# The start of a fused dynamic convolution and FFN: other load order, one read of w_in, other queues for the first rows, bands in pairs

## The chip, the cores and the metric

The kernel runs on one core of one Trainium2 chip. The metric is the device time of one execution in microseconds; several runs are taken and the median is quoted. A profile is one such execution; its span is some 1.9 us shorter than the run's time.

## The reference, cut to what matters

```python
# 8 x 4096 tokens of 192 channels; 8 heads of 24 channels; a 7-tap filter for each token and head
w = softmax(weight_gen, axis=-1)                    # (8, 4096, 8, 7)
x_unf = x_pad[:, idx, :].reshape(B, S, K, H, group)  # the token and the 6 before it
y = einsum('bshk,bskhg->bshg', w, x_unf).reshape(32768, 192)
h = maximum(y @ w_in, 0)                            # w_in 192 x 2048
out = (h * h) @ w_out                               # w_out 2048 x 192, float32 result
```

## The kernel before

The tokens are cut into 64 blocks of 512. For each block: DVE spreads the softmax weights over a band (`bd = wr * mask`), TensorE multiplies x with that band ("conv", PSUM `yp`), ACT copies it out as `y`, TensorE does FFN-in (`h`), ACT takes the relu (`t`), DVE squares it (`g`), and TensorE does FFN-out (`o`) half a block behind. Weights and the first two x blocks come as float32 and are cast on chip; later x blocks are cast by the DMA that POOL issues. Softmax rows are made by ACT and DVE, stored to DRAM (`vd`) and read back shifted (`wr`). Only the first rows go straight from SBUF to SBUF (`wr<-v_first`), as here:

```python
parts[0].load(nc.sync)                 # first softmax rows
x_load_f32(0)
parts[1].load(nc.sync)
load_w_in(0); load_w_in(1)             # each half of the partitions reads all of it: 2 x 384 KB a quarter
s0.exp(0, s0.rh); s1.exp(0, s1.rh)
s0.recip(0, s0.rh); s0.scale(0, s0.rh, nc.vector)
wr_load_sbuf(0, s0)                    # five copies, issued by SyncE
x_cast(0, act); x_load_f32(1)
cast_w_in(0, act); cast_w_in(1, act); load_w_in(2)
s1.recip(0, s1.rh); s1.scale(0, s1.rh, nc.vector)
wr_load_sbuf(1, s0)
load_w_in(3)
for q in range(WO):                    # WO = 4
    load_w_out(q)
    if q == 0:
        s0.store(nc.sync); s1.store(nc.sync)
        wr_load(2)
        for i in (2, 3): cast_w_in(i, pool)
    cast_w_out(q, pool)
parts[2].load(nc.sync)                 # third softmax rows
st_bands(0, BANDS); st_conv(0); st_y_evac(0)
x_cast(1, act); st_bands(1, BANDS)
x_load(2)                              # POOL, behind all the casts above
# ... then the loop over the 64 blocks
```

Each engine takes its own instructions in this order; semaphores order them across engines.

The softmax here doesn't subtract the row's maximum and nothing guards it: scores larger than these inputs give would overflow.

## Time and profile before

| what | value | from |
|---|---|---|
| time, median | 805.39 us (804.39 to 806.07, 4 runs) | runs |
| span of the profiled run, clock granted | 804.9 us, 0.984 | profile |
| TensorE busy from 104 to 780 us | 676 of 676 us | stretches |
| first FFN matmul | 21.02 us | time line |
| block 1's FFN starts | 47.18 us | time line |
| conv of block 3 starts | 59.40 us | time line |
| conv of block 4 ends | 76.46 us | chain |

The prediction shows the lines. The time line gives start, duration, engine, source line, operation and, in brackets, how long the engine was idle and who released it. The idle time that matters is TensorE's, and all of it lies in the first 80 us. The last three rows of the table are marks along the way to the steady part.

### The profile page before, as it was taken

To read this page: it belongs to the slowest core of one execution; us is meant where nothing else is said; L and a number is where in the kernel's file an instruction comes from. 1 tells how busy PE (TensorE), PEld (TensorE's weight loads), DVE (VectorE), ACT (ScalarE), POOL (GpSimd) and SP (SyncE) were. 2 spreads that over 40 slices of the span, in tenths; PEclk is the share of its full clock that TensorE was granted. 3 is DMA by queue.
4 is the path that set the end of the run, shared out by engine and by line. 5 is a ranking of instruction groups with operands and counts; after the bars stand their busy time and mean duration, and the time that the engine had idled before them with its cause. 6 is when DMAs were issued, how large, how long until landed. Compare 5 with 4: busy or idle time off the path is not lost.

```text
span 804.9 us, 32787 instructions
## 1 busy us (share of the span) xinstructions
PE 779.5 (97%) x14900; PEld 682.0 (85%) x14900; DVE 592.9 (74%) x1159; ACT 609.8 (76%) x757; POOL 70.3 (9%) x84
## 2 busy tenths in 40 slices
PE   7678999999999999999999999999999999999998
PEld 3466888888888888888888888888888888888887
DVE  5666878877777777887687777778778777666754
ACT  3556877787787787778778778777877877877785
POOL 3311000010000100001000100000000010000000
PEclk9779999999999999999999999999999999999999
DMA  8773253335343363333634354333533333433111
GB/s 203 192 141 55 62 130 66 70 63 142 62 75 51 63 154 51 68 68 65 140 62 74 52 142 74 51 65 72 142 63 63 70 55 88 74 50 63 49 41 41
DMA packets 125066, 66.70 MB, mean 83 GB/s; under 512 B 84609, under 2 KB 121088, under 8 KB 124160
## 3 DMA queue, kind: packets, MB, share of 16 engines
q1 hardware_dynamic: 83872, 49.18, 22.0%
q0 software_dynamic: 40784, 15.24, 18.0%
q8 instruction: 116, 1.90, 1.0%
q10 hardware_dynamic: 272, 0.20, 0.1%
q14 instruction: 22, 0.18, 0.1%
HBM read 50.31 MB, written 29.36 MB: 99 GB/s over the span
## 4 chain that ended last, share of the span: by engine, by line
PE 92%; DMA 4%; DVE 1%; SPq 1%; issue 1%; POOL 0%; ACT 0%; DVEq 0%; POOLq 0%
PE o L358 43%; PE h L339 43%; PE yp L315 7%; DMA w_st<-in_moe_w_in_dram 1%; DMA xt<-in_x_dram 1%; DMA vd<-v_first 1%; DMA wr<-v_first 1%; DVE bd L274 1%; DMA wo_st<-in_moe_w_out_dram 0%; POOL w_o L130 0%; SPq L114 0%; DVE g L375 0%; DVE v_big L188 0%; ACT ex L167 0%; DVE ssum L175 0%
## 5 line engine op out<-in xcount | busy, mean ns | idle before, releaser
L369 ACT ACTIVATE t<-h 128x1024 f16<-128x1024 f32 x512 | 483.1, 1029 | 10.8 <-PE h L339 10.2
L375 DVE TENSOR_TENSOR g<-t 128x1024 f16<-128x1024 f16 x512 | 346.9, 693 | 172.2 <-ACT t L369 171.9
L339 PE MATMUL h<-y,w_i 64*128 64x256 f16 x6144 | 365.2, 272 | 2.9 <-POOL w_i L118 1.5
L358 PE MATMUL o<-w_o,g 128*128 128x192 f16 x4096 | 360.8, 247 | 2.4 <-POOL w_o L130 2.4
L358 PEld LDWEIGHTS <-g 128*128 128x128 f16 x4096 | 331.9, 98 | 29.4 <-DVE g L375 17.3
L339 PEld LDWEIGHTS <-w_i 64*128 64x128 f16 x6144 | 294.1, 95 | 54.3 <-issue 12.4
L274 DVE TENSOR_TENSOR bd<-wr,mask 128x768 f16<-128x768 f16 (+2 forms) x320 | 170.0, 583 | 12.5 <-DMA wr<-vd 7.6
L328 ACT CAST y<-yp 128x768 f16<-128x768 f32 x64 | 51.1, 798 | 122.8 <-PE yp L315 122.8
L234 POOL DMA_DIRECT2D xt<-in_x_dram x55 | 47.5, 864 | 554.0 <-PE yp L315 519.4
L380 ACT COPY o_sb<-o 128x384 f32<-128x384 f32 x127 | 63.0, 496 | 38.4 <-PE o L358 38.4
L315 PE MATMUL yp<-bd,xt 128*32 128x96 f16 (+17 forms) x4608 | 61.7, 203 | 15.1 <-DMA xt<-in_x_dram 8.7
L315 PEld LDWEIGHTS <-xt 128*32 128x32 f16 (+3 forms) x4608 | 50.6, 91 | 26.6 <-issue 17.3
L175 DVE TENSOR_REDUCE ssum<-ex 128x64 f32<-128x448 f32 (+6 forms) x49 | 26.0, 530 | 16.6 <-ACT ex L167 16.2
L167 ACT ACTIVATE ex<-wg 128x448 f32<-128x448 f32 (+6 forms) x49 | 26.5, 540 | 14.8 <-DMA wg<-in_weight_gen_dram 14.8
L188 DVE TENSOR_TENSOR v_big<-ex,rcp 128x112 f16<-128x112 f32 (+3 forms) x192 | 32.8, 235 | 1.6
L180 DVE RECIPROCAL rcp<-ssum 128x64 f32<-128x64 f32 (+6 forms) x49 | 23.3, 476 | 1.7
L414 PE MATMUL wp<-warm 128*128 128x512 f16 x52 | 13.2, 422 | 1.3 <-DVE warm L408 1.3
L414 PEld LDWEIGHTS <-warm 128*128 128x128 f16 x52 | 5.5, 107 | 8.6 <-issue 2.5
L226 POOL DMA_DIRECT2D xt<-in_x_dram x7 | 3.9, 559 | 80.9 <-PE yp L315 80.9
L188 DVE TENSOR_TENSOR v_first<-ex,rcp 128x112 f16<-128x112 f32 (+2 forms) x32 | 5.5, 247 | 0.2
L232 POOL DMA_DIRECT2D xt<-in_x_dram x7 | 5.2, 748 | 0.0
L118 ACT CAST w_i<-w_st 128x1536 f16<-128x1536 f32 x2 | 2.9, 1472 | 2.9 <-DMA w_st<-in_moe_w_in_dram 2.9
(16 smaller groups left out, 19.7 us busy)
## 6 DMA issues: line engine op xcount, KB each, us to landing
out_dram<-o_sb SPq DMA_DIRECT2D x63, 384.0 KB, 2.7
xt<-in_x_dram POOLq DMA_DIRECT2D x55, 240.0 KB, 4.3
wg<-in_weight_gen_dram SPq DMA_DIRECT2D x6, 1064.0 KB, 6.4
wr<-vd SPq DMA_DIRECT2D x55, 80.0 KB, 2.9
vd<-v_big SPq DMA_DIRECT2D x7, 512.0 KB, 2.9
w_st<-in_moe_w_in_dram SPq DMA_DIRECT2D x8, 384.0 KB, 8.2
wo_st<-in_moe_w_out_dram SPq DMA_DIRECT2D x4, 384.0 KB, 4.2
xt<-in_x_dram POOLq DMA_DIRECT2D x7, 192.0 KB, 3.8
```

The lines of the kernel that those rows point to most:

```text
L167: nc.scalar.activation(out=self.ex[:, lo:hi].rearrange("p r g k e -> p (r g) k e"), in_=self.wg[:, lo:hi].rearrange("p r (g e) k -> p (r g ...
L175: nc.vector.tensor_reduce(out=ssum.rearrange("p r g e -> p (r g) e"), in_=self.ex[:, lo:hi].rearrange("p r g k e -> p (r g) e k"), axis=Ax ...
L188: eng.tensor_tensor(out=bass.AP(tensor=v.tensor, offset=v.offset + lo * H * SL + lo % SL * 2 + g * SL * 2, ap=[list(v.ap[0]), [H * SL + 2, ...
L234: eng.dma_start(out=dst, in_=rows(src, t0 + BASE, width))
L274: nc.vector.tensor_tensor(out=bd_t[j][:, H * lo : H * hi].rearrange("p (g m c) -> p g m c", g=HP, c=2 * SL), in0=wr_t[j][:, i].unsqueeze(2 ...
L315: nc.tensor.matmul(out=yp_t[j][p0 : p0 + m, col + a : col + b], lhsT=x_t[j][:, i, 32 * q : 32 * q + m], rhs=bd[:, h // 2, h % 2, a - lo : ...
L328: nc.scalar.copy(out=y, in_=yp_t[j][:, 0 : NK * TH].rearrange("p (k c) -> p k c", k=NK))
L339: nc.tensor.matmul(out=h[:, half, jj, :], lhsT=w_i[r0 : r0 + RT, k, fc * P : (fc + 1) * P], rhs=y_t[j][r0 : r0 + RT, k, :], start=(jj == 0 ...
L358: nc.tensor.matmul(out=o[half][:, cc * Dm : (cc + 1) * Dm], lhsT=g_t[(j, fp)][:, half, jj, cc * P : (cc + 1) * P], rhs=w_o[:, fc, :], star ...
L369: nc.scalar.activation(out=t1, in_=h_t[(j, fp)], func=ActF.Relu)
L375: nc.vector.tensor_tensor(out=g, in0=t1, in1=t1, op=AluOp.mult)
L380: copy(out=o_sb_t[j][:, half], in_=o_t[j][half][:, 0 : 2 * Dm])
```

## The change

Its intent is to fill TensorE sooner: the loads needed first go first, w_in crosses the DMA engines once, small copies leave SyncE's queue, block 2's x leaves the back of POOL's queue, and two equal band tiles share one DVE op. The core of the diff, with cuts (the notes behind # and the line in brackets are mine):

```diff
+    def load_w_in(q):                       # q = 0, 1: halves
+        nc.sync.dma_start(out=w_sa[q], in_=moe_w_in[0:P, c])
         for r0 in (0, RT):
-            nc.sync.dma_start(out=w_st[q][r0 : r0 + RT], in_=src[:, :, c])
+            nc.sync.dma_start(out=w_sb[q][r0 : r0 + RT], in_=moe_w_in[P:D, c])
+    def cast_w_in(q, straight, crossed):
+        straight(out=w_i[:, 0, c], in_=w_sa[q])
+        crossed(out=w_i[RT:P, 1, c], in_=w_sa[q][0:RT])
+        crossed(out=w_i[0:RT, 1, c], in_=w_sa[q][RT:P])
+        straight(out=w_i[:, 2, c], in_=w_sb[q])
...
-    BASE = -32                              # bands of 96, 104, 104, 96, 112 tokens
+    BASE = -24                              # bands of 104, 104, 104, 104, 96
+            groups = ((0,), (1,), (2, 3)) if j % NBB == 0 else ((0, 1), (2, 3))
...
+        spin(38)                            # warm-up matmuls, 52 before
+        s0.load(nc.sync)
+        s1.load(nc.sync)
         x_load_f32(0)
         load_w_in(0)
         load_w_in(1)
...
+        wr_load_sbuf(s0, (0, 2, 1, 3, 4), (nc.scalar, nc.gpsimd))
+        s0.store(nc.scalar)
+        cast_w_in(0, act, pool)
+        wr_load(1)
+        x_load_f32(1)
+        load_w_out(0)
+        (block 0: bands, conv), spin(4), st_y_evac(0)
+        s1.scale(0, s1.rh, nc.vector)
+        s1.store(nc.sync)
+        cast_w_in(1, pool, pool)
+        x_cast(1, pool)
+        wr_load(2)
+        x_load(2)                           # ahead of the w_out casts now
+        load_w_out(1)
+        for q in range(WQ):                 # two halves, four quarters before
+            cast_w_out(q, pool)
+        s2.load(nc.sync)
```

More of the change, by code (lines that the diff above doesn't have):

```diff
@@ L58 @@
     STEP = 104
-    BASE = -32
+    BASE = -24
     starts = [BASE + STEP * i for i in range(NT)]
-    bounds = [0, 96, 200, 304, 400, TB]
-    shifts = [lo - s for lo, s in zip(bounds, starts)]
+    bounds = [0, 104, 208, 312, 416, TB]
     AluOp = mybir.AluOpType
@@ L69 @@
     p_wg = ctx.enter_context(tc.tile_pool(name="p_wg", bufs=2))
-    p_ex = ctx.enter_context(tc.tile_pool(name="p_ex", bufs=2))
+    p_one = ctx.enter_context(tc.tile_pool(name="p_one", bufs=1))
     p_st = ctx.enter_context(tc.tile_pool(name="p_st", bufs=2))
@@ L102, in band_mask @@
             )
-    WQ = 4
-    WO = 4
-    w_st, wo_st, x_st = {}, {}, {}
+    WQ = 2
+    w_sa, w_sb, wo_st, x_st = {}, {}, {}, {}
     def load_w_in(q):
-        src = moe_w_in.rearrange("(k p) f -> p k f", p=RT)
-        c = slice(q * Dff // WQ, (q + 1) * Dff // WQ)
-        w_st[q] = p_st.tile([P, NK, Dff // WQ], f32, name="w_st")
-        for r0 in (0, RT):
-            nc.sync.dma_start(out=w_st[q][r0 : r0 + RT], in_=src[:, :, c])
-    def cast_w_in(q, copy):
-        c = slice(q * Dff // WQ, (q + 1) * Dff // WQ)
-        copy(out=w_i[:, :, c], in_=w_st[q])
+        n = Dff // WQ
+        c = slice(q * n, (q + 1) * n)
+        w_sa[q] = p_st.tile([P, n], f32, name="w_sa")
+        w_sb[q] = p_st.tile([P, n], f32, name="w_sb")
+        nc.sync.dma_start(out=w_sa[q], in_=moe_w_in[0:P, c])
+        for r0 in (0, RT):
+            nc.sync.dma_start(out=w_sb[q][r0 : r0 + RT], in_=moe_w_in[P:D, c])
+    def cast_w_in(q, straight, crossed):
+        n = Dff // WQ
+        c = slice(q * n, (q + 1) * n)
+        straight(out=w_i[:, 0, c], in_=w_sa[q])
+        crossed(out=w_i[RT:P, 1, c], in_=w_sa[q][0:RT])
+        crossed(out=w_i[0:RT, 1, c], in_=w_sa[q][RT:P])
+        straight(out=w_i[:, 2, c], in_=w_sb[q])
     def load_w_out(q):
-        n = NF // WO
+        n = NF // WQ
         wo_st[q] = p_st.tile([P, n, Dm], f32, name="wo_st")
@@ L128, in cast_w_out @@
     def cast_w_out(q, copy):
-        n = NF // WO
+        n = NF // WQ
         copy(out=w_o[:, q * n : (q + 1) * n], in_=wo_st[q])
@@ L139, in load @@
             r, rh = self.r, self.rh
-            self.wg = wg = p_wg.tile([P, rh, H, KK], f32, name=f"wg{r}")
+            self.wg = wg = (p_one if r == FIRST[2] else p_wg).tile([P, rh, H, KK], f32, name=f"wg{r}")
             base = weight_gen[self.b, self.t0 : self.t0 + r]
@@ L163, in exp @@
             if lo == 0:
-                self.ex = p_ex.tile([P, self.rh, HP, KK, 2], f32, name=f"ex{self.r}")
+                self.ex = (p_wg if self.r == FIRST[0] else p_one).tile([P, self.rh, HP, KK, 2], f32, name=f"ex{self.r}")
                 self.ssum = p_sm.tile([P, self.rh, HP, 2], f32, name=f"ssum{self.r}")
@@ L221, in rows, with tile_start @@
         )
+    ends = [P * sum(FIRST[: i + 1]) for i in range(len(FIRST))]
+    def tile_start(j, i):
+        t1 = (j % NBB + 1) * TB
+        ends_here = t1 == S or j < NBB and t1 in ends
+        return TB - P if i == NT - 1 and ends_here else starts[i]
     def block_load(j, dst, src, width, eng):
         t0 = (j % NBB) * TB
-        if t0 == 0:
+        first, last = int(t0 == 0), NT
+        if first:
             eng.dma_start(out=dst[:, 0], in_=src[0:P, :])
-            later = rows(src, BASE + STEP, width)
-            later = bass.AP(
-                tensor=later.tensor, offset=later.offset,
-                ap=[later.ap[0], [STEP * width, NT - 1], later.ap[2]],
-            )
-            eng.dma_start(out=dst[:, 1:NT], in_=later)
-        else:
-            eng.dma_start(out=dst, in_=rows(src, t0 + BASE, width))
+        a = t0 + tile_start(j, NT - 1)
+        if a != t0 + starts[-1]:
+            last = NT - 1
+            eng.dma_start(out=dst[:, last], in_=src[a : a + P, :])
+        ap = rows(src, t0 + starts[first], width)
+        ap = bass.AP(
+            tensor=ap.tensor, offset=ap.offset,
+            ap=[ap.ap[0], [STEP * width, last - first], ap.ap[2]],
+        )
+        eng.dma_start(out=dst[:, first:last], in_=ap)
     def x_load(j):
@@ L249, in wr_load, with wr_load_sbuf @@
         wr_t[j] = p_wr.tile([P, NT, HP, SL * 2], f16, name="wr")
-        block_load(
-            j, wr_t[j].rearrange("p t g c -> p t (g c)"), vd_t[j // NBB], H * SL, nc.sync
-        )
-    def wr_load_sbuf(j, s):
-        wr_t[j] = p_wr.tile([P, NT, HP, SL * 2], f16, name="wr")
-        for i in range(NT):
-            t0 = j * TB + (0 if i == 0 and j == 0 else starts[i]) - s.t0
-            nc.sync.dma_start(
-                out=wr_t[j][:, i].rearrange("p g c -> p (g c)"),
+        wr = wr_t[j].rearrange("p t g c -> p t (g c)")
+        block_load(j, wr, vd_t[j // NBB], H * SL, nc.sync)
+    def wr_load_sbuf(s, order, engines):
+        wr_t[0] = p_wr.tile([P, NT, HP, SL * 2], f16, name="wr")
+        for n, i in enumerate(order):
+            t0 = max(starts[i], 0)
+            engines[n % len(engines)].dma_start(
+                out=wr_t[0][:, i].rearrange("p g c -> p (g c)"),
                 in_=s.v[t0 // s.r : (t0 + P) // s.r, HALO : HALO + s.r].rearrange(
@@ L264, in wr_load_sbuf, with st_band @@
             )
-    def st_band(j, i):
-        if i == 0:
+    def st_band(j, tiles):
+        if j not in bd_t:
             bd_t[j] = p_bd.tile([P, H * TB], f16, name="bd")
-        lo, hi = bounds[i], bounds[i + 1]
-        n = hi - lo
-        shift = 0 if i == 0 and j % NBB == 0 else shifts[i]
-        m = mask[:, shift : shift + n]
-        shape = (P, HP, n // SL, 2 * SL)
-        nc.vector.tensor_tensor(
-            out=bd_t[j][:, H * lo : H * hi].rearrange("p (g m c) -> p g m c", g=HP, c=2 * SL),
-            in0=wr_t[j][:, i].unsqueeze(2).broadcast_to(shape),
-            in1=m.rearrange("p (m c) e -> p m (c e)", c=SL).unsqueeze(1).broadcast_to(shape),
+        i = tiles[0]
+        lo, hi, n = bounds[i], bounds[tiles[-1] + 1], bounds[i + 1] - bounds[i]
+        shift = 0 if i == 0 and j % NBB == 0 else lo - tile_start(j, i)
+        shape = (P, HP * len(tiles), n // SL, 2 * SL)
+        nc.vector.tensor_tensor(
+            out=bd_t[j][:, H * lo : H * hi].rearrange(
+                "p (g m c) -> p g m c", g=shape[1], c=2 * SL
+            ),
+            in0=wr_t[j][:, i : tiles[-1] + 1]
+            .rearrange("p t g c -> p (t g) c")
+            .unsqueeze(2)
+            .broadcast_to(shape),
+            in1=mask[:, shift : shift + n]
+            .rearrange("p (m c) e -> p m (c e)", c=SL)
+            .unsqueeze(1)
+            .broadcast_to(shape),
             op=AluOp.mult,
@@ L336, in st_mm1 @@
             fc = 2 * fp + jj
-            for k in range(NK):
+            for slot in range(NK):
                 for half, r0 in enumerate((0, RT)):
+                    k = slot ^ half if slot < 2 else slot
                     nc.tensor.matmul(
                         out=h[:, half, jj, :],
-                        lhsT=w_i[r0 : r0 + RT, k, fc * P : (fc + 1) * P],
+                        lhsT=w_i[r0 : r0 + RT, slot, fc * P : (fc + 1) * P],
                         rhs=y_t[j][r0 : r0 + RT, k, :],
-                        start=(jj == 0 and k == 0), stop=(k == NK - 1),
+                        start=(jj == 0 and slot == 0), stop=(slot == NK - 1),
                         skip_group_check=True,
@@ L390, in o_store, with st_bands @@
         )
-    def st_bands(j, tiles):
+    def st_bands(j, part):
         if j < NBLK:
-            for i in tiles:
-                st_band(j, i)
+            groups = ((0,), (1,), (2, 3)) if j % NBB == 0 else ((0, 1), (2, 3))
+            for tiles in (groups, ((NT - 1,),))[part]:
+                st_band(j, tiles)
     G0, G1 = (0, 1, 2, 3), (4, 5, 6, 7)
     UNIT = 4
-    BANDS = (0, 2, 1, 3, 4)
     with nc.allow_low_precision("fp16 matmul pipeline"), tc.manual_schedule():
@@ L412, with spin @@
         wp = ps_h.tile([P, 2 * TB], f32, name="wp", tag="h")
-        for i in range(52):
-            nc.tensor.matmul(
-                out=wp[:, 0:TB], lhsT=warm[:, 0:P], rhs=warm, start=True, stop=True
-            )
+        def spin(n):
+            for i in range(n):
+                nc.tensor.matmul(
+                    out=wp[:, 0:TB], lhsT=warm[:, 0:P], rhs=warm, start=True, stop=True
+                )
+        spin(38)
         band_mask()
@@ L425, in softmax @@
             s.scale(lo, hi, nc.vector)
-        parts[0].load(nc.sync)
+        s0, s1, s2 = parts
+        s0.load(nc.sync)
+        s1.load(nc.sync)
         x_load_f32(0)
-        parts[1].load(nc.sync)
         load_w_in(0)
         load_w_in(1)
-        s0, s1 = parts[:2]
         s0.exp(0, s0.rh)
         s1.exp(0, s1.rh)
+        x_cast(0, act)
         s0.recip(0, s0.rh)
         s0.scale(0, s0.rh, nc.vector)
-        wr_load_sbuf(0, s0)
-        x_cast(0, act)
-        x_load_f32(1)
-        cast_w_in(0, act)
-        cast_w_in(1, act)
-        load_w_in(2)
-        s1.recip(0, s1.rh)
-        s1.scale(0, s1.rh, nc.vector)
-        wr_load_sbuf(1, s0)
-        load_w_in(3)
-        for q in range(WO):
-            load_w_out(q)
-            if q == 0:
-                s0.store(nc.sync)
-                s1.store(nc.sync)
-                wr_load(2)
-                for i in (2, 3):
-                    cast_w_in(i, pool)
-            cast_w_out(q, pool)
-        parts[2].load(nc.sync)
-        st_bands(0, BANDS)
+        s1.recip(0, s1.rh)
+        wr_load_sbuf(s0, (0, 2, 1, 3, 4), (nc.scalar, nc.gpsimd))
+        s0.store(nc.scalar)
+        cast_w_in(0, act, pool)
+        wr_load(1)
+        x_load_f32(1)
+        load_w_out(0)
+        for i in (0, 2, 1, 3, 4):
+            st_band(0, (i,))
         st_conv_alloc(0)
         st_conv(0)
+        spin(4)
         st_y_evac(0)
-        x_cast(1, act)
-        st_bands(1, BANDS)
-        x_load(2)
+        s1.scale(0, s1.rh, nc.vector)
[3 more added lines that the diff above has]
+        wr_load(2)
+        x_load(2)
+        load_w_out(1)
+        for q in range(WQ):
+            cast_w_out(q, pool)
+        s2.load(nc.sync)
+        st_bands(1, 0)
+        st_bands(1, 1)
         plan = {}
@@ L475, in spread @@
                 lo = hi
-        spread(0, parts[2].rh, (0, 1))
+        spread(0, s2.rh, (0, 1))
         for b in range(1, B):
@@ L480 @@
             spread(b, R + HALO, range(first + (2 if b == 1 else -2), first + 5))
-        rows_of = {0: parts[2]}
+        rows_of = {0: s2}
         for j in range(NBLK):
@@ L499 @@
                 if not late:
-                    st_bands(j + 2, BANDS[0:3])
+                    st_bands(j + 2, 0)
             for fp in G0:
@@ L513 @@
                 st_y_evac(1)
-                st_bands(2, BANDS[0:3])
+                st_bands(2, 0)
             if not late:
-                st_bands(j + 2, BANDS[3:5])
+                st_bands(j + 2, 1)
             if hi and j:
@@ L529 @@
             if late:
-                st_bands(j + 2, BANDS)
+                st_bands(j + 2, 0)
+                st_bands(j + 2, 1)
             if j + 3 < NBLK:
```

## The prediction

> **What bounds the kernel now.** I read four views in this order. First the slices of the page, to see where TensorE is not full; then the stretches with their busy times; then the time line of the first 48 us; then the queue's own waits.
>
> ```profile
> PE   7678999999999999999999999999999999999998
> PEclk9779999999999999999999999999999999999999
> ...
> 104.00:780.00 676.00, 676.00 (x13251) 599.23 (x13248) 514.29 (x996) 535.97 (x672) 48.24 (x59) 1.00 0.39 76
> ```
>
> The first two lines are tenths per 20 us; the third gives, for 104 to 780 us, busy PE, PEld, DVE, ACT, POOL, then granted clock, DMA share and GB/s. TensorE is busy for all of 676 us at full clock, so there only fewer or cheaper matmuls could help. The conv of block 6 starts at 101.39 and that of block 63 at 775.75 in the chain that ended last: 674.36 / 57 = 11.83 us a block. All loss lies in the first four slices. The time line there (start, duration, what; in brackets the idle time before it and its releaser):
>
> ```profile
> 16.77 2.57 DVE L274 TENSOR_TENSOR bd<-wr,mask 128x768 f16<-128x768 f16 x5 [2.11 <-DMA wr<-v_first]
> ...
> 21.02 4.97 PE L339 MATMUL h<-y,w_i 64*128 64x256 f16 x48 [0.89 <-ACT y L328]
> ...
> 29.71 1.48 PE L339 MATMUL h<-y,w_i 64*128 64x256 f16 x24 [1.45 <-POOL w_i L118]
> ...
> 35.00 2.04 PE L358 MATMUL o<-w_o,g 128*128 128x192 f16 x16 [2.38 <-POOL w_o L130]
> ...
> 38.40 0.83 POOL L130 CAST w_o<-wo_st 128x768 f16<-128x768 f32 x1 [2.22 <-DMA wo_st<-in_moe_w_out_dram]
> 39.17 3.59 POOL L234 DMA_DIRECT2D xt<-in_x_dram x4
> 39.98 0.83 ACT L167 ACTIVATE ex<-wg 128x672 f32<-128x672 f32 x1 [7.45 <-DMA wg<-in_weight_gen_dram]
> ...
> 45.77 1.48 PE L315 MATMUL yp<-bd,xt 128*32 128x96 f16 x72 [8.73 <-DMA xt<-in_x_dram]
> ```
>
> Two marks matter: the first FFN matmul at 21.02 (block 0), and block 1's FFN at 47.2, right after the conv at 45.77. Stall-free, the way between them is block 0's FFN-in (2 x 2.73), half its FFN-out (2.75) and two convs (2 x 0.86): 9.9 us. It took 26.2. The 8.73 us wait is the largest: block 2's x is issued by POOL only after all four w_o casts, and the last of those waited for the last w_out load. That load is late because SyncE's queue stops:
>
> ```profile
> SPq L234 <- DMA vd<-v_first: 7.1, 2, 5.4
> SPq L202 <- DVE v_first L188: 2.9, 1, 2.9
> SPq L259 <- DVE v_first L188: 2.8, 1, 2.8
> SPq L123 <- DMA wo_st<-in_moe_w_out_dram: 2.7, 1, 2.7
> ```
>
> (who waited for what: total us, times, longest.) SyncE issues in order, so each of these holds up every load behind it.
>
> **What the Trainium skill says.** "DMA: Bandwidth & Descriptors", section "Issuing engines are not separate DMA queues": all issuers share 16 DMA engines and interleave; its section "Queues, rings and completion order" says that an engine goes round the rows that have work, packet by packet. So the same small copy on another queue need not sit behind SyncE's backlog. The trace shows that backlog: wr copies (80 KB or less) land 2.0 us after issue at best, 8.1 at worst, and the worst are those issued at 8.6 us behind four w_in loads. "TensorE: Matmul & The Clock Gate", Part 1, gives two clock states, half and full, changed by some 3.4 us of idleness or work; the trace has means of 0.70 for 21 to 47.2 us and 1.00 later, so idle gaps are paid twice. "GPSIMD Engine Reference", section 1, lists contention between POOL and a DVE op with two SBUF inputs; the trace agrees: bands are 584 ns in the median, but the one that met POOL's w_in cast took 1773. "VectorE: DVE Perf Modes", rules for authors: lower the count of ops, not the semaphores. In the steady stretch bands take about 552, 586 and 619 ns for 768, 832 and 896 columns: 0.52 ns a column and 150 ns fixed, though neighbours overlap by about 80.
>
> **The change part by part.**
>
> *Bands.* From block 2 on, 5 ops become 3. One of 1664 columns takes 150 + 0.52 x 1664 = 1.02 us, so a block has 2 x 1.02 + 0.55 = 2.59 instead of 0.55 + 2 x 0.59 + 0.55 + 0.62 = 2.90, some 0.15 net of overlaps. DVE is at 514 of 676 us in the steady stretch and no bound: worth nothing there. At the one place where DVE ends the wait (block 4's conv at 74 us, behind softmax, four squares and all five bands, 2.3 us of PE idle) it gives 0.1, while the conv starts later because it needs both wide ops. The conv stays at 72 matmuls, with piece widths 104/104/48 instead of 96/104/56: nothing. The swap of w_in's blocks changes no count either.
>
> *w_in read once.* Before, 8 loads of 384 KB = 3072 KB. After, 2 x 512 + 4 x 256 = 2048 KB. In this trace w_in loads landed 384 KB every 1.1 to 1.8 us (12.1, 13.8, 15.0, 16.5), about 250 KB/us, so 1024 KB fewer are 4.1 us less queue. Price: casts. Per half ACT or POOL does two of 128x1024 and POOL two of 64x1024. POOL took 1.46 us for 1536 columns, so about 1.0 for 1024; the second half is four in a row on POOL, 4 us, and DVE will be held up some 0.6 us for each that meets it (square ops took 1.3 instead of 0.68 beside the w_o casts).
>
> *First rows on other queues.* The five copies cost SyncE 0.6 us each and landed at 16.7 to 17.5. Now three go through ACT after its x cast, two through POOL as soon as v_first is ready (8.5). With both softmax loads ahead of it, x lands at about 9.5 (it was 8.7 behind one); cast to 10.5; ACT issues at 10.5, 11.1, 11.7; landed at about 13 to 14.5; bands done 15.3, conv 15.8. ACT then needs w_in's first half: 1264 + 1024 = 2288 KB down the queue, and before 2032 KB were down at 13.8 and 2416 at 15.0, so about 14.6; the last cast ends at 15.7 and the copy of y at 16.6. First FFN matmul near **17.2** (16.5 to 18.3), not 21.0: 3.8 us. The warm-up of 38 matmuls ends near 11.5 instead of 14.5, so PE still idles 3 to 4 us and probably drops to half clock as before; the four extra ones keep it busy while y is copied.
>
> *The way to 47.2.* From 14.6 SyncE's ring holds w_in's second half (1024 KB), block 1's wr (80), x (480), w_out's first half (768) and the second store (128): 2480 KB. x and w_out went at some 350 KB/us in this trace, w_in at 250: 4.1 + 0.2 + 1.4 + 2.2 + 0.4 = 8.3, hence about 23.5 with delays. POOL has finished w_in's second half by 21 to 22, x of block 1 by 23 and, what matters most, issues block 2's x **at about 23 instead of 39.2**, before the w_o casts; at 4 to 6.5 us to landing it is there by 28. wr of block 2 waits for the second store (23.5), lands near 26, and its bands end at 28.5. PE: FFN-in of block 0 17.2 to 22 (half clock, as before 4.97), conv 1 at 23 to 24, second half to 27, FFN-out to 29.8, conv 2 to 30.7. The third softmax load follows w_out's second half (768 + 616 KB at 400, from 24.5) and lands near 29.5; its exp delays y 2 little. So block 1's FFN starts at about **30.5** instead of 47.2.
>
> *Sum.* 47.2 - 30.5 = 16.7. Of it 3.8 come before the first FFN matmul, the other 12.9 from the way between. Blocks 2 to 4 keep their stall, the rest is full already: 805.0 - 16.7 = **788.3 us**.
>
> **The rivals.** (A) *POOL becomes the bound of the start.* It now has seven casts of about 1 us and two of 1.5 us, in order, ahead of or among the x loads, and they collide with bands and scaling on DVE. For it: the 1773 ns band. Against: POOL was idle for 14.3 us before its first cast. If each of six collisions costs 0.6 on the path, 3.6 us come back: 792. (B) *The SyncE chain store, wr, w_out remains.* Block 1's wr now sits ahead of x and w_out in SyncE's order and waits for the first store, block 2's wr for the second; every microsecond there delays w_out's second half and the third softmax load, after which ACT's in-order exp holds up y 2. For it: the 7.1 us of such waits above. If the store takes the 5.8 us it took before, 791 to 794. (C) *All stalls vanish.* Then 17.2 + 9.9 = 27.1 for the second mark, and 785. (D) *The wait only moves,* from w_out to another load, as the DMA engines are 0.84 busy to 21 us and 0.86 to 47: then just the 1024 KB, about 4 us: 801. I give it little, since their bytes per time were only 204 GB/s against the 350 and more of single loads.
>
> **Range and chances.** A 2% gain means below about 789.1 us. My centre lies 0.8 below; the errors of the first mark (about 1), of the chain to the second (about 2.5), and of the clock's half-speed windows (1.7 each, 3.4 us at half) add to about 3. Hence 784.5 to 793.5, faster 0.58, same 0.41, slower 0.01.
>
> **What would show it.** In the changed profile: first FFN matmul at 16.5 to 18.3; POOL's issue of block 2's x at 22 to 25; block 1's FFN at 29 to 33; from 104 us on PE full with 11.8 us a block; band groups of 1664 columns near 1.02 us; w_in bytes 2 MB; the stall before conv 4 still there at about 2 to 4 us. I am wrong if PE is slower per block in the steady part, if ACT's own DMA issues or POOL's casts delay the first FFN matmul to 20 or later, or if a wait of over 4 us on w_o, wr or exp stands in place of the 8.73.

## The result, and the profile after

The changed kernel takes **793.63 us** in the median (791.54 to 795.07, 4 runs) against 805.39. The ratio is 0.9853, with a 95% interval of 0.9827 to 0.9879. (A ratio here is the mean time of one kernel's runs over that of the other's of the same rounds, so not quite the ratio of the medians.) That is 11.8 us less, where 16.7 were predicted; the time lies just above the predicted range, and within 2% of before.

First the slices of the page and the steady stretch of the changed kernel, same columns as before:

```profile
PE   5998999999999999999999999999999999999998
PEclk9999999999999999999999999999999999999999
...
104.00:780.00 676.00, 676.00 (x13200) 601.23 (x13199) 504.11 (x884) 534.00 (x673) 49.87 (x65) 1.00 0.39 74
```

TensorE is full from 104 us on, as it was. The second and third slices are full now (9 tenths, 6 and 7 before); the fourth stays at 8. The first one has less work in it than before (5 tenths, 7 before). The time line of the start shows where this comes from:

```profile
8.56 1.95 ACTq L275 DMA_DIRECT2D wr<-v_first  x3
...
15.12 5.48 DVE L290 TENSOR_TENSOR bd<-wr,mask 128x832 f16<-128x832 f16 x5 [4.83 <-DMA wr<-v_first]
...
23.01 2.79 PE L364 MATMUL h<-y,w_i 64*128 64x256 f16 x48
...
25.11 0.89 POOL L251 DMA_DIRECT2D xt<-in_x_dram  x1
...
33.75 1.48 PE L364 MATMUL h<-y,w_i 64*128 64x256 f16 x24
34.84 0.83 ACT L173 ACTIVATE ex<-wg 128x672 f32<-128x672 f32 x1 [2.81 <-DMA wg<-in_weight_gen_dram]
...
36.40 1.75 PE L364 MATMUL h<-y,w_i 64*128 64x256 f16 x24 [1.17 <-ACT y L352]
...
46.51 0.91 PE L339 MATMUL yp<-bd,xt 128*32 128x104 f16 x72
```

The reader is to see three things. The first FFN matmul starts **later** than before (23.01 against 21.02): the bands begin sooner (15.12 against 16.77), but five of them take 5.48 us where they took 2.57, so they end 1.3 us later, and the four warm-up matmuls then hold the first FFN matmul 0.8 us past the copy of y. POOL issues block 2's x at 25.11 instead of 39.17, and block 1's FFN starts at 33.75 instead of 47.18. And a new hole of 1.17 us stands in that FFN, after the first 24 of its 96 matmuls: the next ones start at 36.40, as ACT had to run exp, which waited for its load, before it could copy out block 2's y (y's PSUM source and h take turns in the same buffers).

The chain of work that ended last (start, duration, what) names what led to that hole:

```profile
8.56 6.46 DMA wr<-v_first
...
15.12 5.48 DVE bd L290 x5
20.60 1.38 DVE v_first L194 x8
...
22.00 3.20 DMA vd<-v_first
...
26.19 8.62 DMA wg<-in_weight_gen_dram
...
35.57 0.78 ACT y L352
```

Row copies, bands, scaling of the second rows, their store, and only then, as SyncE issues in order, the third softmax load, which took 8.62 us to land.

| mark | before | after | gain so far |
|---|---|---|---|
| first FFN matmul | 21.02 | 23.01 | -2.0 |
| block 1's FFN | 47.18 | 33.75 | 13.4 |
| conv of block 3 | 59.40 | 46.51 | 12.9 |
| conv of block 4 ends | 76.46 | 63.37 | 13.1 |
| end of the span | 804.9 | 791.0 | 13.9 |

The two profiled runs took 806.78 and 792.94 us, so this pair differs by 13.8; of the gap to the 11.8 of the medians, 1.4 is the profiled run of before being slow and 0.7 the other one being fast. The last 0.8 us of the table arise in the steady part, to which I had given no gain. They lie in the conv: from block 6 on its span on TensorE is 0.841 to 0.842 us in the mean in every kernel built from the changed one, single and w_in_twice included, and 0.855 to 0.856 in before and before_x2; 57 blocks of that difference make nearly all of the 0.8 us. So neither the pairs nor the reading of w_in gives it. It goes with the new band bounds, which all those kernels keep; no run undoes them alone.

### The profile page after: what moved, and what is told of

Its sections match the earlier page's. It is cut to its first block, busy times and chain, and to the rows that moved or that the text cites. A ratio compares the mean times of both kernels' runs of the same rounds, so it can differ in the third digit from the quotient of the medians.

```text
span 791.0 us, 32666 instructions
## 1 busy us (share of the span) xinstructions
PE 773.3 (98%) x14890; PEld 679.7 (86%) x14890; DVE 586.7 (74%) x1040; ACT 605.4 (77%) x756; POOL 81.8 (10%) x98
## 3 DMA queue, kind: packets, MB, share of 16 engines
q0 software_dynamic: 40992, 15.28, 18.5%
## 4 chain that ended last, share of the span: by engine, by line
PE 93%; DMA 3%; DVE 2%; ACT 1%; issue 0%; SPq 0%; ACTq 0%; DVEq 0%
PE o L383 44%; PE h L364 43%; PE yp L339 6%; DMA wg<-in_weight_gen_dram 1%; DVE bd L290 1%; DMA wr<-v_first 1%; DMA x_st<-in_x_dram 1%; DMA vd<-v_first 0%; DVE g L400 0%; ACT t L394 0%; DVE v_big L194 0%; ACT ex L173 0%; DVE v_first L194 0%; DVE ssum L181 0%; DVE rcp L186 0%
## 5 line engine op out<-in xcount | busy, mean ns | idle before, releaser
L290 DVE TENSOR_TENSOR bd<-wr,mask 128x1664 f16<-128x1664 f16 (+2 forms) x201 | 163.4, 844 | 11.2 <-DMA wr<-vd 6.2
L251 POOL DMA_DIRECT2D xt<-in_x_dram x62 | 51.2, 826 | 460.4 <-PE yp L339 437.0
L339 PE MATMUL yp<-bd,xt 128*32 128x104 f16 (+13 forms) x4608 | 59.9, 203 | 10.6 <-DVE bd L290 10.5
L245 POOL DMA_DIRECT2D xt<-in_x_dram x9 | 5.0, 552 | 85.2 <-PE yp L339 85.2
L241 POOL DMA_DIRECT2D xt<-in_x_dram x7 | 3.8, 541 | 77.5 <-PE yp L339 77.5
L136 POOL CAST w_o<-wo_st 128x1536 f16<-128x1536 f32 x2 | 3.7, 1826 | 5.7 <-DMA wo_st<-in_moe_w_out_dram 5.7
```

The costliest lines, as they stand in the source:

```text
L251: eng.dma_start(out=dst[:, first:last], in_=ap)
L290: nc.vector.tensor_tensor(out=bd_t[j][:, H * lo : H * hi].rearrange("p (g m c) -> p g m c", g=shape[1], c=2 * SL), in0=wr_t[j][:, i : tile ...
L339: nc.tensor.matmul(out=yp_t[j][p0 : p0 + m, col + a : col + b], lhsT=x_t[j][:, i, 32 * q : 32 * q + m], rhs=bd[:, h // 2, h % 2, a - lo : ...
```

## The experiments

Each kernel was built from the changed one unless said otherwise, ran in rounds against the kernel before on the same chip, and gave the right result. The changed kernel was run again as a control. One thousandth of ratio is 0.8 us.

| run | median us | ratio to before, 95% interval | first FFN matmul | conv of block 3 |
|---|---|---|---|---|
| changed | 793.63 | 0.9853 (0.9827 to 0.9879) | 23.0 | 46.5 |
| after_again | 794.06 | 0.9850 (0.9835 to 0.9865) | 24.2 | 47.9 |
| x2_last | 798.94 | 0.9937 (0.9914 to 0.9959) | 25.0 | 53.0 |
| before_x2 | 801.46 | 0.9933 (0.9906 to 0.9960) | 19.2 | 50.6 |
| w_in_twice | 794.96 | 0.9866 (0.9850 to 0.9883) | 20.8 | 48.3 |
| single | 792.68 | 0.9838 (0.9816 to 0.9861) | 24.3 | 48.0 |
| dve_casts | 792.17 | 0.9853 (0.9834 to 0.9872) | 21.2 | 46.3 |
| w1_act | 793.65 | 0.9869 (0.9838 to 0.9900) | 18.7 | 47.3 |
| wr_sync | 790.97 | 0.9831 (0.9811 to 0.9851) | 17.8 | 44.6 |
| s2_early | 792.05 | 0.9852 (0.9831 to 0.9873) | 23.6 | 45.6 |
| wr_s2 | 790.39 | 0.9828 (0.9792 to 0.9865) | 16.5 | 43.6 |
| late_mid | 788.51 | 0.9803 (0.9771 to 0.9836) | 23.2 | 46.6 |
| combo | 785.33 | 0.9761 (0.9731 to 0.9790) | 18.5 | 44.5 |

The last two columns are from one profile each; two profiles of the changed kernel differ by 1.2 and 1.4 us there, so less than that is not to be read from one of them.

### The control: after_again

> The changed kernel once more, unedited, as the control of this batch. All theories: ratio to before 0.983 to 0.988, that is 792 to 795 us, with the half-clock time of each run (share of granted clock below 1) explaining about half of a run's distance from the fastest.

The ratio came out as 0.9850. The clock granted was 0.990 to 0.991 in all four runs, for 793.35 to 794.35 us. In the first set it ranged from 0.989 (795.07 us) to 0.995 (791.54 us). The traces record the clock as 1 or as 0.5, the latter in stretches of 3.4 us or a multiple of it (but for the one that the end of a span cuts). So, as an estimate, 0.006 of clock are 9.5 us of 791 at half clock, which cost up to 4.7 us where TensorE has work. The spread was 3.5.

### Where block 2's x stands in POOL's order: x2_last, before_x2

```diff
 # x2_last
-        x_load(2)
         load_w_out(1)
         for q in range(WQ):
             cast_w_out(q, pool)
+        x_load(2)
```

> Undoes one part of the change: POOL issues block 2's x after both w_out casts again, as before; all else as changed. Theory (most of the gain is that x load leaving the back of POOL's queue): the issue moves from 25.1 to about 35.3 us, x lands near 40, the conv of block 2 moves from 32.8 to about 40, the conv of block 3 from 46.5 to about 53, and the time rises by 5 to 7 us, to 799 to 801. Rival (the load was hidden, or the third softmax load bounds anyway): under 1.5 us.

It cost what was expected. TensorE's time line of that run:

```profile
39.29 0.91 PE L339 MATMUL yp<-bd,xt 128*32 128x104 f16 x72 [3.70 <-DMA xt<-in_x_dram]
```

Block 2's conv again waits for x and starts at 39.3 instead of 32.8; the ratio rises from 0.985 to 0.9937, about 7 us.

```diff
 # before_x2: the kernel BEFORE, one line moved
                 for i in (2, 3):
                     cast_w_in(i, pool)
+                x_load(2)
...
-        x_load(2)
```

> The kernel before with one line moved: POOL issues block 2's x right after its second w_in cast, ahead of the four w_out casts. Theory (that place in POOL's order held most of what was to gain): the issue moves from 39.2 to about 29.7 us, x lands near 34, block 2's conv moves from 45.8 to about 37 (after the wait for w_o), exp of the third rows then holds up y of block 2 to about 41.6, the conv of block 3 starts at 51 to 53 instead of 59.4, and the time falls by 6 to 8 us, to about 797 to 799. Rival (queue bytes bound the start, so that x only trades places with w_out): under 3 us.

TensorE's time line of that run has block 2's conv with no wait for x any more, and the wait for y that was expected:

```profile
34.24 0.92 PE L315 MATMUL yp<-bd,xt 128*32 128x96 f16 x72
35.09 1.48 PE L339 MATMUL h<-y,w_i 64*128 64x256 f16 x24
39.40 2.74 PE L339 MATMUL h<-y,w_i 64*128 64x256 f16 x24 [2.82 <-ACT y L328]
```

One line moved in the old kernel brings 0.0067, some 5.4 us by the ratios and 4.1 by the medians. That is less than the 6 to 8 expected; its profile, with 797.45 us the fastest of its four runs (the others 801.4 to 802.4), had conv of block 3 at 50.55, even a little better than expected. The direction and the mechanism hold in both kernels: **this one place in a queue is worth some 5 to 7 of the 12 us, by the ratios.**

### Reading w_in once: w_in_twice

```diff
-        straight(out=w_i[:, 0, c], in_=w_sa[q])         # and three more casts a half
+        copy(out=w_i[:, :, c], in_=w_st[q])             # two casts a half, from quarters
+        # load: 2 x 384 KB a quarter, as before; four buffers, so no load waits for a cast
```

> Undoes one part: w_in is read twice again (quarters of 2 x 384 KB, 3072 KB in all), two 1536-column casts per half on ACT and then on POOL, the first FFN in the old order of blocks; all else as changed, with a buffer for each quarter so that no load waits for a cast. Theory (reading once is worth its 1024 KB in the shared queue): row copies land 1.5 to 2 us later, everything behind the second half 4 us later, the time rises by 3 to 4.5 us. Rival (the extra POOL casts and their collisions eat the saved bytes): four POOL casts of 1.3 us become two, bands take 4 us at most instead of 5.5, and the time rises by under 1.5 us or falls.

Only 0.0016 slower than the control, 1.3 us, and the intervals overlap: the rival's size, if it is a difference at all. The 1024 KB are paid, as the second half lands at 22.8 instead of 16.8 us. But the first FFN matmul comes at 20.8, earlier than with one read: POOL's first cast of that half starts only at 19.18, after the five bands, which take 2.57 us. The saved bytes and the added casts nearly cancel, as far as these runs tell.

### Bands in pairs: single

```diff
-            groups = ((0,), (1,), (2, 3)) if j % NBB == 0 else ((0, 1), (2, 3))
+            groups = ((0,), (2,), (1,), (3,))
```

> Undoes the grouped bands: one tile per DVE op again (four of 832 columns and one of 768 a block), order 0, 2, 1, 3, 4; all else as changed. Theory (DVE bounds nothing after 100 us, so the grouping is worth nothing there): within 0.7 us of the changed kernel of the same batch, DVE busy up by 5 to 8 us; block 4's conv starts about 1 us earlier and ends within 0.2 us of where it did. Rival (the grouping carries a part of the gain): 1.5 us or more slower.

The intervals of 0.9838 and 0.9850 overlap: the pairs are worth nothing here. The groups of DVE from 104 to 780 us (count | busy us, mean ns | idle us before), with pairs and then without:

```profile
L290 DVE TENSOR_TENSOR bd<-wr,mask 128x1664 f16<-128x1664 f16 (+2 forms) x172 | 138.7, 835 | 3.3 <-DMA wr<-vd 3.1
```

```profile
L290 DVE TENSOR_TENSOR bd<-wr,mask 128x768 f16<-128x768 f16 x276 | 145.7, 576 | 6.2 <-DMA wr<-vd 6.2
```

The pairs do save DVE 7 us of 676 (the shape named is the commonest in a sample). DVE is not waited for there.

### Why the first FFN matmul is late: dve_casts, w1_act, wr_sync

```diff
 # dve_casts
-        cast_w_in(1, pool, pool)
+        cast_w_in(1, vec, vec)
```

> The four casts of w_in's second half go from POOL to DVE, after the scaling of the second rows, so POOL casts no longer meet block 0's bands. Theory (the collision of POOL casts with DVE bands moved the first FFN matmul to 23.0): the five bands take about 2.6 us instead of 5.5 and the first FFN matmul starts at 20 to 20.8. For the end: theory 1, the chain second store, wr of block 2, w_out, third softmax load bounds the second mark, and the store then sits behind w_out in the queue until about 24.3 instead of 25.2: only 0.5 to 1.5 us of gain (792 to 793). Theory 2, the late first FFN matmul passes to the end in full: 2.5 to 3 us (791).

The groups of the stretch from 11.5 to 21 us, changed kernel first, then this one:

```profile
L290 DVE TENSOR_TENSOR bd<-wr,mask 128x832 f16<-128x832 f16 x4 | 5.0, 1310 | 4.8 <-DMA wr<-v_first 4.8
...
L124 POOL CAST w_i<-w_sb 128x1024 f16<-128x1024 f32 x1 | 1.3, 1282 | 0.1
```

```profile
L290 DVE TENSOR_TENSOR bd<-wr,mask 128x832 f16<-128x832 f16 x4 | 2.1, 586 | 6.0 <-DMA wr<-v_first 6.0
```

With no POOL cast beside it a band takes 586 ns, beside one 1310 in the mean: the collision is shown, and it was worth 2.9 us at the bands. Yet the end did not move (0.9853), and even theory 1's 0.5 us did not appear. The edit does not decide between the theories: DVE now has the four casts ahead of block 1's bands, and in this trace block 1's conv waits 0.34 + 0.65 + 1.14 us for x and for those bands, which gives a part of the gain away.

```diff
 # w1_act: 512 KB of w_in's second half on ACT's queue, behind the row copies
-        nc.sync.dma_start(out=w_sa[q], in_=moe_w_in[0:P, c])
+        (nc.scalar if q else nc.sync).dma_start(out=w_sa[q], in_=moe_w_in[0:P, c])
...
-        load_w_in(1)
         s0.exp(0, s0.rh)
...
         s0.store(nc.scalar)
+        load_w_in(1)
```

> The row copies stay on ACT's and POOL's queues, as changed; only the bytes given to the DMA engines ahead of them are cut: the 512 KB of w_in's second half go to ACT's queue behind the copies, and just 256 KB of that half are issued by SyncE before them. Theory (a copy lands when everything issued before it, on any queue, has landed): the copies land at 13.2 to 14.2 us instead of 15.0 to 15.9, each within 0.6 us behind the last load issued before them, and the first FFN matmul starts 1 to 2.5 us earlier than 23.0 to 24.2. Rival (what counts is their own queue, or their own cost of some 6 us): unchanged landing at 15 us or later. End of the kernel: 0 to 1.5 us earlier.

```diff
 # wr_sync: the copies back on SyncE, ahead of w_in's second half
-        load_w_in(1)
...
-        wr_load_sbuf(s0, (0, 2, 1, 3, 4), (nc.scalar, nc.gpsimd))
+        wr_load_sbuf(s0, (0, 2, 1, 3, 4), (nc.sync,))
+        load_w_in(1)
```

> The five row copies go back to SyncE, but ahead of the loads of w_in's second half. Theory (landing is set by the bytes already given to the shared DMA engines, whichever queue issued the copy): they land at 13 to 14 us instead of 15.0 to 15.9 although SyncE issues them 0.6 us apart, bands are done by about 17 as POOL's later casts do not meet them, first FFN matmul at 18 to 19.5 instead of 23.0; w_in's second half lands 2 us later, so the end gains 0 to 2 us. Rival (own queues did bypass the backlog and the 6.4 us are the cost of the copies themselves): landing at 15 us or later, and the time rises.

From the DMA records of these traces, in us:

| run | queue of the copies | first issued | last load issued before it landed | first copy landed |
|---|---|---|---|---|
| before | SyncE | 8.56 | 16.47 | 16.67 |
| changed | ACT and POOL | 8.56 | 14.51 | 15.02 |
| dve_casts | ACT and POOL | 8.30 | 15.80 | 15.97 |
| s2_early | ACT and POOL | 8.23 | 14.96 | 15.13 |
| w1_act | ACT and POOL | 8.68 | 13.22 | 13.58 |
| wr_sync | SyncE | 8.31 | 11.79 | 11.97 |

Whichever queue issues it, a copy is reported landed just behind the loads that were issued ahead of it. (In one run, single, it came 0.4 us ahead of the last of them.) Taking bytes away moves it, also where the queue stays the same (w1_act). The theory holds; the rival falls. In the changed kernel the data packets of ACT's copies ran from 11.7 to 14.0 us, so they were neither prompt nor last; the report came a further microsecond on.

The first FFN matmul of w1_act came 4.3 us earlier than in the changed kernel, more than the 1 to 2.5 expected, as its bands met no cast either (586 ns). The end gained nothing there (0.9869, wide interval), and its time line shows why: the hole in block 1's FFN, 1.17 us in the changed kernel, has grown.

```profile
35.52 2.05 PE L364 MATMUL h<-y,w_i 64*128 64x256 f16 x24 [2.87 <-ACT y L352]
```

In wr_sync the ratio fell by 1.5 us. An earlier first FFN matmul thus passes to the end in small part only. Even the 1.5 us are not surely the copies': the stall before block 4's conv is as long in wr_sync as before (2.73 + 0.62), but in its profile no half-clock window follows it. The chain after that conv, changed kernel and then wr_sync:

```profile
63.37 4.39 PE h L364 x48
```

```profile
61.46 2.73 PE h L364 x48
```

That is 1.7 of the 3.7 us by which the two profiles differ, and wr_s2's profile lacks the window too. Whether the edits or the chance of where the clock's windows fall did this, no run tells; combo and late_mid, below, have no such stall and compare without it.

### What bounds the end of the start: s2_early, wr_s2

```diff
 # s2_early
         load_w_out(0)
+        s2.load(nc.sync)
...
-        s2.load(nc.sync)
```

> The third softmax load is issued right after the first half of w_out, so it does not wait in SyncE's order for the second store. Theory 1 (exp of these rows, waiting for that load in ACT's order, holds up y of block 2): exp runs before 30 us, y of block 2 at about 33.8 instead of 35.6, conv of block 3 at 44 to 44.7 instead of 46.5, time down by 1.8 to 2.6 us, to about 791.3. Rival (w_out's second half, pushed back by 616 KB, becomes the wait): gain under 0.7 us and PE waits for w_o.

ACT's time line in this run:

```profile
32.56 0.91 ACT L173 ACTIVATE ex<-wg 128x672 f32<-128x672 f32 x1
34.58 0.80 ACT L352 CAST y<-yp 128x768 f16<-128x768 f32 x1 [1.11 <-PE yp L339]
```

Exp no longer waits, and y of block 2 waits only for TensorE. The wait is gone as expected, the expected gain is not: 0.9852, no difference; in the profile conv of block 3 came 1.0 us sooner, which is less than two profiles of one kernel differ by. TensorE ran from the first FFN matmul at 23.6 to that conv with no wait left, so the late first matmul had become the bound. With the wait of 2.87 us in w1_act this fits two bounds side by side, where either hides the other.

```diff
 # wr_s2 = wr_sync, and:
         x_load(2)
+        s2.load(nc.sync)
         load_w_out(1)
```

> Row copies on SyncE ahead of w_in's second half, and the third softmax load ahead of w_out's second half. Theory (two bounds in series-parallel: the first FFN matmul, and the chain second store, SyncE, third softmax load, exp; removing one alone gave 0 to 2 us): first FFN matmul at 17.5 to 19, no wait of PE for y of block 2, conv of block 3 at 43.3 to 44.3, 789 to 790.5. Rival (w_out's second half becomes the wait): PE waits for w_o over 1 us and the time stays at 791.

Taken together: first FFN matmul at 16.5, no wait for y, conv of block 3 at 43.6, 790.39 us. Against the control that is 1.8 us by the ratios, but the intervals overlap, and against wr_sync (0.9831) nothing is to be told. TensorE now waits 4.5 us before block 1's conv, for POOL's cast of block 1's x, which stands behind the casts of w_in's second half: that is the longest wait left before block 4's stall. My rival, w_out, was not it.

```profile
23.75 1.47 PE L339 MATMUL yp<-bd,xt 128*32 128x104 f16 x72 [4.48 <-POOL xt L263]
```

### A stall that the change left: late_mid, combo

```diff
 # late_mid
-            if not late:
-                st_bands(j + 2, 1)
+            if late:
+                st_bands(j + 2, 0)
+            st_bands(j + 2, 1)
             if hi and j:
                 s = rows_of[nb]
                 softmax(s, lo, hi)
...
-            if late:
-                st_bands(j + 2, 0)
-                st_bands(j + 2, 1)
```

> A place that the change left as it was: block 4's bands are made in the middle of block 2, ahead of the softmax piece, instead of at its end. Theory (PE idles 2.7 + 0.6 us before block 4's conv because DVE does softmax and four squares first, and the half clock after it costs up to 1.7 more): no idle time before that conv, no half-clock window near 61 us, 3.3 to 5 us less than the changed kernel, so 788.5 to 790.5. Rival (the squares, made later, become the wait): under 1 us.

TensorE's time line before block 4's conv, changed kernel and then this one:

```profile
61.62 0.23 PE L339 MATMUL yp<-bd,xt 128*32 128x104 f16 x2 [2.73 <-DVE bd L290]
62.46 0.91 PE L339 MATMUL yp<-bd,xt 128*32 128x56 f16 x70 [0.62 <-DVE bd L290]
```

```profile
58.85 0.90 PE L339 MATMUL yp<-bd,xt 128*32 128x104 f16 x72
```

The 3.35 us of waiting are gone, and so is the half-clock window that began at 63.8 us in the changed kernel's profile. The ratio fell from 0.985 to 0.9803, about 3.8 us, as expected (the intervals only touch). The DVE order had cost more than most of the change's parts are worth.

combo is late_mid, wr_sync and the third softmax load of wr_s2.

> All three: row copies on SyncE first, the third softmax load ahead of w_out's second half, block 4's bands in the middle of block 2. If the gains add: 785 to 787.5, faster than both kernels, ratio to before 0.975 to 0.979. If DMA bytes bound the start and the stall only moves: 788 or more.

It took **785.33 us** (784.93 to 785.44), ratio 0.9761 with an interval of 0.9731 to 0.9790: faster than both kernels, and 3.2 us faster than late_mid beside it, with no run of the one in the range of the other (784.93 to 785.44 against 787.64 to 790.08). So the two chains of the start, taken away together, are worth about 3 us at the end.

## Why the prediction was wrong

**What held.** The bound and the place of all gain were read rightly: TensorE full from 104 us on, and the loss in the first four slices. Block 2's x behind the w_out casts was the largest single part, as said, and x2_last and before_x2 show it at 5 to 7 us. Band pairs were worth nothing, the pair op took 1.02 us as worked out, and the stall before conv 4 stayed, at 3.35 us. That the time lies only 0.1 us outside the range says little: the runs of this one kernel spread over 3.5 us.

**First step that failed: "First rows on other queues", and with it the mark of 17.2 us.** It was read from the packet-by-packet sharing that copies on ACT's and POOL's queues "need not sit behind SyncE's backlog". They were issued even sooner than I took (8.56, as x was cast by 8.97 and not 10.5), but landed at 15.0 to 15.9, not 13 to 14.5. The backlog counts whatever the queue, as w1_act and wr_sync show. No run shows their own queues to be worth anything at the landing (none has them on SyncE behind the same loads); putting them on SyncE ahead of 1024 KB was worth 3 us there. The prediction's own sign of being wrong, a first FFN matmul at 20 or later, came true with 23.0.

**Second: the price of the casts.** I had seen the collision of POOL casts with DVE and priced it at some 0.6 us for each that meets a DVE op, then left it out of "bands done 15.3". As the bands came late they met the four casts of w_in's second half: bands of 832 columns took 1310 ns in the mean instead of 586, and the five took 5.48 us. This is rival A, at 2.9 us on the bands, shown by dve_casts. The four extra warm-up matmuls, meant to keep the clock up, ran at half clock after it (1.77 us) and held the first FFN matmul some 0.8 us past the copy of y.

**Third, and this is in the chain that ended last: "The way to 47.2".** The first mark came 5.8 us late, yet dve_casts and w1_act, which brought back 1.8 and 4.3 us of that, gained nothing at the end. Behind it stood another chain, rival B. Block 2's x went out at 25.1, not 23, since POOL's cast of block 1's x took 3.4 us beside back-to-back bands. The second store landed at 25.2, not 23.5. And the third softmax load landed at 34.8, not 29.5: I had put 768 and 616 KB at 400 KB/us, where with block 2's x beside them some 1860 KB took 8.6 us, about 216 KB/us. So "its exp delays y 2 little" failed, and the hole at 36.40 opened. (B's 791 to 794 holds the measured time, but by other terms: the store took 3.2 us and not B's 5.8, the load 8.6.) This wait alone did not set the end either, as s2_early took it away for nothing; with the late first matmul gone too, combo is 3.2 us below late_mid, of the 3.8 us missed here. By marks: block 1's FFN 3.2 us late (33.75 against 30.5), conv of block 3 3.8 late (46.5 against 42.7, which is 30.5 plus the old 12.2).

**The sum.** Predicted 16.7; 3.8 of that did not come, 1.0 came unforeseen after conv 3 (0.2 to the end of conv 4, 0.8 in the steady part): 13.9, as the pair of profiles has. The medians put it at 11.8, as that pair was a favourable one by 2.1 us. I had taken every mark from one profile of before whose run was 1.4 us slow. The 0.8 belong to the conv pieces, to which the prediction gives "nothing". It also misread the clock of before as 1.00 after 47.2 us: the stretches have 0.92 from 47.2 to 80.

**Reading w_in once** was priced at 4.1 us of queue. The runs give 1.3 at the end, not clear of noise; in w_in_twice's trace the casts that no longer meet the bands take the rest back.

**What stays open.** The parts undone here are 5 to 7 us (x) and 1.3 (w_in), with nothing from pairs or own queues; some 4 us of the 12 are in the rest (w_out in two halves with a buffer each, fewer waits in SyncE's order, fewer half-clock windows, 0.8 in the conv pieces) and were not taken apart. What the copies' order alone is worth stays open too, for the clock's windows.

## What to carry to other kernels

Ask for each load which instruction stands in front of it in its issuer's order, before asking how many bytes it has: moving one issue ahead of two casts was worth more than saving a megabyte. Do not count on a small copy to overtake a backlog by another queue, as it did not here; issue the backlog after it. And when two chains bound a start side by side, removing the wait in one can show nothing until the other goes, so test them together, and look for stalls that the change did not touch.

## What the Trainium skill lacked or had wrong

- "DMA: Bandwidth & Descriptors", section "Queues, rings and completion order", has no number for how long a small copy waits behind another queue. What it says was right, and I had read half of it. Beside the sharing by packets it says that the semaphore increment is a strongly ordered write that lands after every earlier write of that DMA engine, "across its queues". The traces agree: the copies on ACT's and POOL's queues were reported 0.2 to 0.5 us behind loads of SyncE's queue (15.02 after 14.51, 13.58 after 13.22), about 1 us after their last data packet (the store behind them on ACT's queue: 0.5, from 15.75 to 16.24). No run separates this ordering from plain waiting in the engines, since the first data packet came only 3.1 us after issue. The consequence is on the page, in the section that the prediction cites first: issuing on several engines saves only the time of issuing.
- "GPSIMD Engine Reference", section 1, names the contention with DVE but gives no size, and no other page has one for a DVE multiply beside a POOL cast. Here a DVE multiply of 832 columns took 1310 ns in the mean beside POOL casts and 586 alone; the casts took about 1280 instead of 1038. A POOL cast of 960 columns took 3403 ns beside three DVE multiplies in a row, and 991 in s2_early, where it met the short scaling ops.
- No page gives the rate of a load with w_in's rows (pieces of 2048 or 4096 bytes from rows 8 KB apart). In the DMA records of the changed kernel SyncE's queue, then almost all w_in, moved 147 to 311 GB/s in each microsecond from 6 to 15, with the row copies beside it from 11.7 on; x and w_out, in pieces of 768 bytes, 314 to 361 GB/s from 20 to 23 us. No run isolates the size of the pieces.
- "TensorE: Matmul & The Clock Gate", Part 1, puts the cost of the clock's ramp at under 1% of a typical span and calls it run-variable. Both agree here, and there is nothing wrong in it; but under 1% is as much as the parts under test: the granted clock ranged from 0.989 to 0.995 over runs of one kernel and went with a spread of 3.5 us of 791, and the same stall of 3.35 us was followed by a half-clock window in the changed kernel's profile and by none in wr_sync's.
